# A linear-attention and feed-forward kernel on one core: the same steps in a new program order, 94 of them on another engine

## The chip, the cores and the metric

The kernel runs on one core of a Trainium2 chip. The metric is the device time of one execution in microseconds (us); the median of three runs before the change is 522.75 us (522.26 to 524.58).

## What is computed

Two stages follow one another. The first is a linear attention with a decaying state, for 4 batches, 8 heads, 768 time steps and a head dimension of 48. The second is a feed-forward layer over all 3072 tokens, from 384 to 2048 channels and back.

```python
for t in range(S):
    cur = np.einsum('bhd,bhe->bhde', u[None] * kt, vt)
    y[:, :, t] = np.einsum('bhd,bhde->bhe', rt, state + cur)
    state = w[None, :, :, None] * state + np.einsum('bhd,bhe->bhde', kt, vt)
...
h = x @ w_in
sp = np.maximum(h, 0.0) + np.log1p(np.exp(-np.abs(h)))
g = h * erf(sp)
return (g @ w_out).astype(np.float32)
```

## The kernel before

**Chunks.** Time is cut into chunks of 128 steps; 6 chunks of 4 batches make 24 chunk steps g = 0 to 23, each with all 8 heads. For a chunk the inputs r, k and v are loaded (`load_a`, `load_b`: words `L`), scaled by powers of the decay (`K`, `R`, `N`: lines 218, 222, 226), multiplied on TensorE into the in-chunk matrix A (`A`, L301), masked into two tiles am whose diagonal was prepared before (`Q` L263, L266, L270, then `M` L281 or L283, then `P` L309), and multiplied with v and with the state sbd into y (`Y`, L330). `D` (L353) with `S` (L366, L368, L372) moves the state on. `X` puts y into x in two parts, a rounded one and its residue (L375, L378; for chunks 0 to 3 through L389 and L392).

**Blocks.** Four chunks make a block x of 512 tokens; there are 6. For each block the feed-forward layer goes over 16 tiles of 128 hidden channels: 96 steps n. `f` (L411) is nine matmuls of 512 columns into h; `a b z c d e g` is the activation (ScalarE L418, L422, L431, L435, L439; VectorE L427, L443); `h` and `l` split the result into two parts (L449 on ScalarE, L454 on VectorE); `p` (L471) is nine matmuls into the three accumulators. The tile h has three buffers. Blocks 0 and 1 take turns: tiles 0 to 7 of both, then 8 to 15 of both; their sums go through memory in between (`O`).

**Weights.** The weights arrive as 64-bit words and are turned into two float parts on the chip, in 16 groups `Cwg` (w = 0 for w_in, 1 for w_out; g = 0 to 7; a group serves two hidden tiles). Part a (L123) is ScalarE's, b, c and d are three passes of VectorE over 128x768 (L125, L127, L130), e is a copy on ScalarE (L133), and f a subtraction (L135) on VectorE or GpSimd. All groups share one work tile wt and two raw tiles. `F` loads a group. By their shapes a raw tile is 768 KB, `load_a` brings 512 KB, `load_b` 608 KB (224 KB for chunks 0 and 1), and ub is 192 KB.

**The order.** `ORDER` (from line 701) is a table of words written out by hand or by a planner; the loop at lines 517 to 596 takes them one after another and issues each word's instructions on their engines. So the table is the program order of every engine's queue. The letter is the step, the number its chunk or hidden tile, and the last sign the engine of the steps that can run on several: none is VectorE, `+` is GpSimd, `*` is ScalarE (line 518):

```python
eng = {"+": nc.gpsimd, "*": nc.scalar}.get(x[-1], nc.vector)
```

`W2` issues two dummy matmuls (`keep_warm`, L92); ahead of the table 16 more are issued. Loads wait on SyncE's queue, in the table's order, for their buffers.

Of the kernel before, what the change touches and what calls it, by code (L numbers as in the profile page):

```python
# [36 lines left out]
V0, K0, R0, AW = 1024, 1472, 1856, 2240  # L37
# [669 lines left out]
M50* N4+ z2 M51 A5 C02b C02c C02d K6+ c2 f3 d2 a3 e2 e1 C02e p0x p0y p0z P50 g2 h2 b3 Q6a P51 g1 z3 C02f+ Q6b+ R6+ Y4
X4a D4 h1 c3 X4b l2 Q6c l1 C11a d3 L7a L7b F03 Y5 f4 f5 M60* X5a M61* e3 C11b C11c N5 C11d S4b S4a X5b C11e F12 R7+
C11f g3 Q7a+ K7+ Q7b+ a4 a5 b5 z5 b4 C03a c5 A6 p1 z4 P60 P61 p2 D5 Y6 C03b C03c C03d c4 d5 h3 l3 d4 e5 L8a L8b F13 g5
C03e X6a h5 e4 S5b S5a X6b Q7c p3 C03f+ M70+ C12a M71* A7 l5 g4 f6 f7 h4 a6 P70 C12b C12c C12d P71 Y7 l4 b6 C12e a7 b7  # L710
C12f z6 z7 C13a c6 c7 d6 X7a d7 e6 C13b C13c C13d X7b g6 N6+ K8+ Q8a+ F14 p4 p5 f8 e7 h6 g7 h7 C13e l6 a8 C13f l7 Q8b+
b8 z8 C14a C14b f9 a9 c8 b9 d8 C14c R8 S4c+ N7+ z9 Q8c M80+ e8 g8 p6 F04 p7x O70a c9 d9 h8 C14d l8 f10 a10 p7y e9 b10
g9 z10 M81+ A8 p7z f11 p8x P80 P81 N8+ O71a C14e c10 C14f+ S4d O70b F05 h9 O71b l9 O72a d10 e10 a11 b11 C05a D6 D7 p8y
p8z p9 f12 g10 h10 S7a S6a z11 C05b C05c c11 d11 e11 C05d C05e g11 h11 l10 l11 S7b O72b L10a L10b L9a L9b F07 a12 b12
C05f+ S6b z12 f13 f14 p10 C04a C04b C04c C04d p11 Y8 c12 a13 b13 d12 F15 e12 g12 z13 a14 C04e C04f b14 z14 h12 l12
# [118 lines left out]
```

## Time and profile before

| | |
|---|---|
| median of 3 runs | 522.75 us (522.26 to 524.58) |
| the profiled execution, its own time | 521.7 us |
| its span | 520.0 us |
| TensorE busy | 500.6 us (96%) |
| ScalarE busy | 392.8 us (76%) |
| VectorE busy | 361.2 us (69%) |
| GpSimd busy | 142.0 us (27%) |
| memory read and written | 41.09 MB and 6.29 MB |
| mean granted TensorE clock | 0.995 of full speed |

The span runs from the first to the last event of the core; the execution's own time lies 1.7 us above it. PE is TensorE, DVE is VectorE, ACT is ScalarE, POOL is GpSimd, SP is SyncE. A busy time is the part of the span in which an engine has an instruction under way; neighbouring instructions of one engine can overlap by some hundredths of a microsecond.

### The profile page before, as it was taken

What the parts mean: (1) busy time and instruction counts of PE and PEld (TensorE: products, weight loads), DVE (VectorE), ACT (ScalarE), POOL (GpSimd) and SP (SyncE); (2) the same over time, 40 slices, a digit from 0 to 9 for tenths busy, and PEclk for the clock granted to TensorE, in tenths of its full rate; (3) what the DMA queues carried; (4) which work ended last, traced back from release to release, by engine and by line L of the source; (5) the groups of instructions that cost most, each with busy time, mean ns of one, the idle gap of its engine ahead of it and who ended that gap; (6) DMA issues with size and microseconds to landing.
All of it is one profiled execution on the core that took longest, in us unless ns stands there. A gap on an engine that the chain in (4) does not pass through costs nothing.

```text
span 520.0 us, 11077 instructions
## 1 busy us (share of the span) xinstructions
PE 500.6 (96%) x4479; PEld 393.6 (76%) x4482; DVE 361.2 (69%) x636; ACT 392.8 (76%) x720; POOL 142.0 (27%) x139
## 2 busy tenths in 40 slices
PE   8888899999999999999999999999999999999995
PEld 4766667778777787877778787787777886888884
DVE  7999999997798865766467765657758655444452
ACT  2667859998998776777775877667787687887892
POOL 5444670423570323145312420113422000000000
PEclk9998999999999999999999999999999999999999
DMA  7853543561621142430203200514030000010001
GB/s 281 296 195 110 210 152 121 201 221 63 224 87 40 43 136 84 150 110 0 89 3 126 110 6 0 179 29 151 21 129 1 1 1 3 0 62 0 1 0 66
DMA packets 13993, 48.16 MB, mean 93 GB/s; under 512 B 1776, under 2 KB 2160, under 8 KB 13936
## 3 DMA queue, kind: packets, MB, share of 16 engines
q1 hardware_dynamic: 13936, 47.39, 26.0%
q8 instruction: 37, 0.61, 0.5%
q14 instruction: 20, 0.16, 0.1%
HBM read 41.09 MB, written 6.29 MB: 91 GB/s over the span
## 4 chain that ended last, share of the span: by engine, by line
PE 86%; DVE 7%; issue 2%; ACT 2%; POOL 1%; ACTq 0%; DVEq 0%; POOLq 0%
PE acc L471 39%; PE h L411 35%; PE y L330 5%; PE A L301 4%; PE dummy L92 1%; PE ds L353 1%; DVE wt L127 1%; DVE wt L130 1%; DVE am L309 1%; DVE wt L125 1%; DVE h L443 1%; DVE s L427 0%; POOL wil L135 0%; DVE att L218 0%; ACT x L375 0%
## 5 line engine op out<-in xcount | busy, mean ns | idle before, releaser
L411 PE MATMUL h<-x,wih 128*128 128x512 f32 x576 | 184.9, 402 | 2.4 <-DVE sbd L366 1.2
L411 PEld LDWEIGHTS h<-x,wih 128*128 128x128 f32 x576 | 107.4, 189 | 31.7 <-ACT x L375 1.3
L471 PE MATMUL acc<-gh,woh 128*128 128x512 f32 x288 | 117.0, 406 | 0.0
L411 PE MATMUL h<-x,wil 128*128 128x512 f32 x288 | 114.3, 397 | 0.0
L471 PE MATMUL acc<-gh,wol 128*128 128x512 f32 x288 | 114.2, 397 | 0.0
L471 PE MATMUL acc<-gl,woh 128*128 128x512 f32 x288 | 114.0, 396 | 0.0
L443 DVE SCALAR_TENSOR_TENSOR h<-s,h 128x512 f32<-128x512 f32 x96 | 66.3, 693 | 47.6 <-ACT s L439 47.1
L427 DVE SCALAR_TENSOR_TENSOR s<-s,h 128x512 f32<-128x512 f32 x96 | 65.1, 682 | 46.8 <-ACT s L422 46.6
L454 DVE TENSOR_TENSOR gl<-h,gh 128x512 fp32r<-128x512 f32 x96 | 66.1, 688 | 35.5 <-ACT gh L449 34.4
L449 ACT CAST gh<-h 128x512 fp32r<-128x512 f32 x96 | 56.0, 583 | 41.6 <-DVE h L443 31.0
L418 ACT ACTIVATE s<-h 128x512 f32<-128x512 f32 x96 | 56.8, 595 | 25.0 <-PE h L411 24.7
L431 ACT ACTIVATE s<-s 128x512 f32<-128x512 f32 x96 | 59.6, 627 | 20.2 <-DVE s L427 19.8
L471 PEld LDWEIGHTS acc<-gh,woh 128*128 128x128 f32 x288 | 54.2, 188 | 14.6 <-issue 0.8
L411 PEld LDWEIGHTS h<-x,wil 128*128 128x128 f32 x288 | 54.4, 189 | 13.1
L471 PEld LDWEIGHTS acc<-gh,wol 128*128 128x128 f32 x288 | 54.2, 188 | 13.2
L471 PEld LDWEIGHTS acc<-gl,woh 128*128 128x128 f32 x288 | 54.3, 189 | 12.0
L435 ACT ACTIVATE s<-s 128x512 f32<-128x512 f32 x96 | 60.2, 628 | 1.7
L422 ACT ACTIVATE s<-s 128x512 f32<-128x512 f32 x96 | 60.1, 630 | 1.8
L439 ACT ACTIVATE s<-s 128x512 f32<-128x512 f32 x96 | 60.1, 630 | 1.6
L283 POOL TENSOR_TENSOR am<-idents,q 128x512 f32<-128x512 f32 x24 | 27.9, 1168 | 98.9 <-DVE q L270 49.0
L309 DVE COPY_PREDICATED am<-mask,A 64x128 f32<-64x128 uint32 (+2 forms) x108 | 38.3, 389 | 2.3 <-PE A L301 1.5
L330 PE MATMUL y<-am,att 128*32 128x128 f32 x768 | 26.7, 273 | 4.0 <-DVE am L309 2.3
(89 smaller groups left out, 482.2 us busy)
## 6 DMA issues: line engine op xcount, KB each, us to landing
att<-in_att_dram SPq DMA_DIRECT2D x22, 608.0 KB, 5.7
att<-in_att_dram SPq DMA_DIRECT2D x24, 512.0 KB, 4.1
raw<-in_win_dram SPq DMA_DIRECT2D x8, 768.0 KB, 6.1
raw<-in_wout_dram SPq DMA_DIRECT2D x8, 768.0 KB, 4.6
out_dram<-o SPq DMA_DIRECT2D x18, 256.0 KB, 2.1
part<-o SPq DMA_DIRECT2D x6, 256.0 KB, 2.4
o<-part SPq DMA_DIRECT2D x6, 256.0 KB, 4.4
att<-in_att_dram SPq DMA_DIRECT2D x2, 224.0 KB, 7.4
```

Source lines behind the costliest of these rows:

```text
L330: nc.tensor.matmul(out=y[r:r + 32, q, :], lhsT=lhsT, rhs=rhs, start=r not in new, stop=True, skip_group_check=True)
L411: nc.tensor.matmul(out=h, lhsT=w[:, f, q, :], rhs=x[:, xi, q, :], start=k == 0, stop=k == 8)
L418: nc.scalar.activation(out=s1, in_=e["h"], func=AF.Tanh, bias=FB0, scale=FA0)
L422: nc.scalar.activation(out=s1, in_=s1, func=AF.Tanh, bias=FB1, scale=FA1)
L427: nc.vector.scalar_tensor_tensor(out=e["s"], in0=e["s1"], scalar=FG, in1=e["h"], op0=ALU.mult, op1=ALU.add)
L431: nc.scalar.activation(out=s, in_=s, func=AF.Tanh, bias=FB2, scale=FA2)
L435: nc.scalar.activation(out=s, in_=s, func=AF.Square, bias=FB3, scale=FA3)
L439: nc.scalar.activation(out=s, in_=s, func=AF.Square, bias=FB4, scale=FA4)
L443: nc.vector.scalar_tensor_tensor(out=h, in0=ff[n]["s"], scalar=FC, in1=h, op0=ALU.subtract, op1=ALU.mult, reverse0=True)
L449: nc.scalar.copy(out=e["gh"], in_=e["h"])
L454: eng.tensor_tensor(out=e["gl"], in0=e["h"], in1=e["gh"].bitcast(F32), op=ALU.subtract)
L471: nc.tensor.matmul(out=acc[e], lhsT=w[:, f, es], rhs=g, start=first and i == 0, stop=last and i == 2)
```

## The change

Only the table changes: the loop, the steps and all shapes stay. The new table holds the same words in another order, but for three `W2` of nine, which are gone (6 dummy matmuls). 94 words carry another engine sign: of the steps `N`, `K`, `R`, `Qa`, `Qb`, `M`, `S` and `C..f`, 42 go from GpSimd to VectorE and 5 to ScalarE, 36 come to GpSimd from VectorE and 7 from ScalarE, and 4 change between VectorE and ScalarE. Two lines of each table:

```diff
-L0a W2 W2 W2 L1a U0 L0b L2a L2b L3a L3b L1b F00 B0 B0* F01 K0 R0 A0 K1 G0 R1 V0 A1 G1 P00 K2+ V1 Q0 P01 P10 T0 H0 N0*
-t0 N1* Y0 D0 D1 Q2a+ R2 Q2b Q3a Q3b+ R3+ Q2c P11 M20+ Q1 M21* S0d Q3c Y1 C00a X0a M30* L4a L4b S0c S1c S1d C00b N3
+L0a L0b L1a F00 L2a L2b L1b L3a U0 L3b B0 B0* C00a R2+ R0 K0 A0 G0 V0 R1 K1 F01 G1 C00b P00 P01 C00c Q0 A1 W2 V1 C00d
+Q1 P10 P11 R3+ N0* H0 C00e Y0 D0 W2 T0 X0a N1* t0 Y1 D1 L5a L5b Q2a+ S0c Q3a Q2b Q2c M20* S0d K2 X1a M21* A2 L4a Q3b
...
```

**SyncE, the first loads.** Before, all of the first four chunks is loaded ahead of the first weights (raw00 is group C00):

```order
L68 DMA att0_167<-in_att_dram 128x1024
L68 DMA att1_178<-in_att_dram 128x1024
L81 DMA ub_90<-in_u_dram 128x384
L72 DMA att0_167<-in_att_dram 128x448
L68 DMA att2_182<-in_att_dram 128x1024
L72 DMA att2_182<-in_att_dram 128x1216
L68 DMA att3_185<-in_att_dram 128x1024
L72 DMA att3_185<-in_att_dram 128x1216
L72 DMA att1_178<-in_att_dram 128x448
L107 DMA raw00_189<-in_win_dram 128x768
```

After:

```order
L68 DMA att0_167<-in_att_dram 128x1024
L72 DMA att0_167<-in_att_dram 128x448
L68 DMA att1_170<-in_att_dram 128x1024
L107 DMA raw00_172<-in_win_dram 128x768
L68 DMA att2_174<-in_att_dram 128x1024
L72 DMA att2_174<-in_att_dram 128x1216
L72 DMA att1_170<-in_att_dram 128x448
L68 DMA att3_178<-in_att_dram 128x1024
L81 DMA ub_90<-in_u_dram 128x384
L72 DMA att3_178<-in_att_dram 128x1216
```

The first weights move from the tenth to the fourth of these loads, and the loads of chunks 2 and 3 and of ub stand behind them.

**GpSimd, from the preparation of chunk 7 to that of chunk 8** (att7 and att8 are the chunks' inputs, wol and wil the second weight parts, am the masks). Before:

```order
L263 TENSOR_TENSOR att7_807<-att7_807,ub_90 128x384
L218 TENSOR_TENSOR att7_807<-att7_807,wk_116 112x512
L266 TENSOR_TENSOR att7_807<-att7_807 128x384
L135 TENSOR_TENSOR wil_95<-wt03_897,wih_94 128x768
L283 TENSOR_TENSOR am7_0_1023<-idents_98,q7_1011 128x512
L226 TENSOR_TENSOR att6_579<-att6_579,wkn_146 128x384
L218 TENSOR_TENSOR att8_997<-att8_997,wk_116 112x512
L263 TENSOR_TENSOR att8_997<-att8_997,ub_90 128x384
L266 TENSOR_TENSOR att8_997<-att8_997 128x384
L372 TENSOR_TENSOR sbd_147<-sbd_147,wp_114 48x4x48
L226 TENSOR_TENSOR att7_807<-att7_807,wkn_146 128x384
```

After:

```order
L263 TENSOR_TENSOR att7_811<-att7_811,ub_90 128x384
L135 TENSOR_TENSOR wol_97<-wt11_861,woh_96 128x768
L218 TENSOR_TENSOR att7_811<-att7_811,wk_116 112x512
L226 TENSOR_TENSOR att7_811<-att7_811,wkn_146 128x384
L226 TENSOR_TENSOR att6_554<-att6_554,wkn_146 128x384
L283 TENSOR_TENSOR am7_0_987<-idents_98,q7_984 128x512
L283 TENSOR_TENSOR am7_1_989<-idents_98,q7_984 128x512
L135 TENSOR_TENSOR wol_97<-wt12_1038,woh_96 128x768
L266 TENSOR_TENSOR att8_976<-att8_976 128x384
L218 TENSOR_TENSOR att8_976<-att8_976,wk_116 112x512
```

The five steps on chunk 8, the state and chunk 7 that followed one another are split: those of chunk 7 come earlier, and those of chunk 8 stand behind the subtraction for weight group C12 (wt12), which needs VectorE's passes over that group.

**VectorE, the passes over C12 and the masks of chunk 7** (wt12 is C12's work tile, am7 the masks). Before:

```order
L454 TENSOR_TENSOR gl_5_1050<-h5_851,gh_5_1005 128x512
L443 SCALAR_TENSOR_TENSOR h4_841<-s2_4_927,h4_841 128x512
L309 COPY_PREDICATED am7_0_1023<-mask_99,A7_0_1032 128x512
L125 TENSOR_SCALAR wt12_1025<-wt12_1025 128x768
L127 SCALAR_TENSOR_TENSOR wt12_1025<-raw12_881,wt12_1025 128x768
L130 SCALAR_TENSOR_TENSOR wt12_1025<-raw12_881,wt12_1025 128x768
L309 COPY_PREDICATED am7_1_1027<-mask_99,A7_1_1033 128x512
L454 TENSOR_TENSOR gl_4_1111<-h4_841,gh_4_1073 128x512
L135 TENSOR_TENSOR wol_97<-wt12_1025,woh_96 128x768
```

After:

```order
L135 TENSOR_TENSOR wil_95<-wt03_949,wih_94 128x768
L454 TENSOR_TENSOR gl_4_1034<-h4_873,gh_4_1020 128x512
L427 SCALAR_TENSOR_TENSOR s2_5_1036<-s1_5_1017,h5_951 128x512
L125 TENSOR_SCALAR wt12_1038<-wt12_1038 128x768
L127 SCALAR_TENSOR_TENSOR wt12_1038<-raw12_978,wt12_1038 128x768
L130 SCALAR_TENSOR_TENSOR wt12_1038<-raw12_978,wt12_1038 128x768
L427 SCALAR_TENSOR_TENSOR s2_6_1053<-s1_6_1050,h6_1024 128x512
L309 COPY_PREDICATED am7_0_987<-mask_99,A7_0_991 128x512
L309 COPY_PREDICATED am7_1_989<-mask_99,A7_1_992 128x512
```

The subtraction for C03 (wil), on which the matmuls of hidden tiles 6 and 7 rest, is now VectorE's and stands eight instructions ahead of the second mask of chunk 7; before it was GpSimd's.

## Rows read from the trace of the kernel before

**Rows 1.** Busy time by stretches: from-to, length, then each engine's busy us (instructions), PEclk.
```profile
60.00:80.00 20.00, 17.36 (x253) 13.54 (x253) 19.22 (x26) 13.87 (x27) 11.77 (x10) 1.00 0.43 144
80.00:100.00 20.00, 20.00 (x176) 15.31 (x172) 18.99 (x32) 19.41 (x35) 5.60 (x4) 1.00 0.43 151
...
320.00:360.00 40.00, 39.69 (x441) 31.56 (x441) 25.98 (x49) 28.52 (x52) 6.78 (x7) 1.00 0.34 117
...
400.00:440.00 40.00, 39.16 (x366) 30.97 (x358) 23.57 (x45) 29.09 (x55) 2.36 (x2) 1.00 0.01 2
```

**Rows 2.** Chain that ended last, in order of time: start us, us, what.
```profile
44.76 3.18 PE h L411 x9
...
247.00 2.10 PE h L411 x9
249.11 1.67 PE y L330 x56
```

**Rows 3.** Timeline of PE around 79 us: start us, us, what [idle before <-releaser].
```profile
79.14 1.07 PE L330 MATMUL y<-am,att 128*32 128x128 f32 x28 [2.25 <-DVE am L309]
...
80.13 0.50 PE L471 MATMUL acc<-gh,woh 128*128 128x512 f32 x1
```

**Rows 4.** Timeline of DVE, 54 to 82 us: the passes of two weight groups and neighbours.
```profile
54.42 0.55 DVE L125 TENSOR_SCALAR wt<-wt 128x768 int32<-128x768 int32 x1
55.00 0.96 DVE L127 SCALAR_TENSOR_TENSOR wt<-raw,wt 128x768 int32<-128x768 int32 x1
...
56.35 3.03 DVE L130 SCALAR_TENSOR_TENSOR wt<-raw,wt 128x768 int32<-128x768 int32 x1
...
72.26 2.35 DVE L125 TENSOR_SCALAR wt<-wt 128x768 int32<-128x768 int32 x1
74.65 1.67 DVE L127 SCALAR_TENSOR_TENSOR wt<-raw,wt 128x768 int32<-128x768 int32 x1
76.35 2.10 DVE L130 SCALAR_TENSOR_TENSOR wt<-raw,wt 128x768 int32<-128x768 int32 x1
78.37 0.71 DVE L309 COPY_PREDICATED am<-mask,A 128x512 f32<-128x512 uint32 x1
```

**Rows 5.** Timeline of POOL, 71 to 78 us, first and last of five.
```profile
71.93 1.29 POOL L218 TENSOR_TENSOR att<-att,wk 112x512 f32<-112x512 f32 x1
...
76.64 0.99 POOL L226 TENSOR_TENSOR att<-att,wkn 128x384 f32<-128x384 f32 x1
```

**Rows 6.** Timeline of DVE, 28 to 47 us: first and last of four more long instructions.
```profile
28.98 1.77 DVE L218 TENSOR_TENSOR att<-att,wk 112x512 f32<-112x512 f32 x1
...
44.80 1.63 DVE L125 TENSOR_SCALAR wt<-wt 128x768 int32<-128x768 int32 x1
```

**Rows 7.** Groups by line and shape: line engine op xcount | busy us, mean ns | idle before.
```profile
L443 DVE SCALAR_TENSOR_TENSOR h<-s,h 128x512 f32<-128x512 f32 x96 | 66.3, 693 | 47.6 <-ACT s L439 47.1
L427 DVE SCALAR_TENSOR_TENSOR s<-s,h 128x512 f32<-128x512 f32 x96 | 65.1, 682 | 46.8 <-ACT s L422 46.6
L135 DVE TENSOR_TENSOR wol<-wt,woh 128x768 fp32r<-128x768 f32 x5 | 4.8, 961 | 0.9 <-ACT woh L133 0.9
L283 DVE TENSOR_TENSOR am<-idents,q 128x512 f32<-128x512 f32 x6 | 4.3, 716 | 0.0
L226 DVE TENSOR_TENSOR att<-att,wkn 128x384 f32<-128x384 f32 x7 | 3.8, 551 | 0.0
L231 DVE TENSOR_TENSOR att<-att 112x512 f32<-112x512 f32 x2 | 1.4, 688 | 0.0
```

**Rows 8.** Timeline of POOL, its first large step.
```profile
10.19 1.54 POOL L218 TENSOR_TENSOR att<-att,wk 112x512 f32<-112x512 f32 x1 [4.99 <-DMA att<-in_att_dram]
```

**Rows 9.** Busy time of PE alone by stretches of 2 us: PE busy, PEclk.
```profile
44.00:46.00 2.00, 2.00 (x17) 0.50 0.83 335
```

**Rows 10.** Timeline of PE and DVE: six dummies, and masks late in the span.
```profile
39.16 1.89 PE L92 MATMUL dummy<-warm 128*128 128x512 bf16 x6 [0.27 <-PE h L411]
...
433.13 1.94 DVE L309 COPY_PREDICATED am<-mask,A 128x256 f32<-128x256 uint32 x6
```

More of the change, by code (lines that the diff above doesn't have):

```diff
@@ L707 @@
[L707 to L711, printed above, removed]
@@ new lines @@
+C00f Q3c M30* M31* K3+ P20 N3+ A3 X0c X1c Q5a K5 X1b X0b C01a P30 P31 D3 Y3 L4b P21 Y2 Q5b+ S1d Q5c S1c Q4a N2+ D2 X3a
+X2a R4+ C01b Q4b K4 S3d Q4c M40+ M41+ C01c S3c S2d C01d S2c F02 L6a L6b F10 X3c X2c X3b X2b W2 f0 A4 f1 M50* M51* a0
+b0 z0 C01e C01f f2 Q6a N4 P40 P41 Q6b+ R5+ A5 W2 K6+ R6+ c0 d0 a1 e0 b1 g0 z1 a2 b2 z2 h0 l0 C10a P50 C10b C10c C10d
+P51 Q6c f3 c2 c1 d2 e2 Y4 D4 W2 C10e X4a d1 C10f C02a N5 X4b C02b C02c S4a C02d Y5 W2 p0x p0y p0z L7a F11 F03 L7b e1
+a3 X5a b3 C02e R7+ C02f+ X5b g1 S4b h1 M60* M61+ A6 g2 z3 l1 C11a c3 d3 h2 e3 P60 C11b C11c C11d P61 f4 C11e a4 D5 Y6
@@ new lines @@
+p1 Q7a+ C11f+ b4 S5b g3 l2 X6a C03a f5 p2 K7+ z4 S5a X6b C03b L8a F12 C03c Q7b N7+ C03d Q7c N6+ M70+ M71+ A7 c4 h3 d4
+e4 l3 g4 a5 C03e h4 b5 C03f f6 l4 z5 C12a c5 C12b C12c C12d L8b F14 F13 d5 a6 b6 z6 P70 e5 P71 g5 f7 C12e a7 p3 Y7
+C12f+ Q8a b7 c6 z7 h5 d6 l5 e6 X7a c7 d7 e7 Q8b+ Q8c g6 X7b K8+ M80+ M81+ g7 p4 p5 f8 h6 l6 C13a C13b h7 C13c C13d l7
+a8 b8 z8 C13e f9 f10 c8 a9 d8 b9 z9 S4d+ C13f+ R8+ e8 C14a F05 g8 C14b C14c p6 c9 a10 d9 h8 C14d l8 p7x p7y p7z A8 e9
+C14e b10 O70a O70b F04 g9 O71a h9 f11 C14f+ P80 z10 l9 C05a a11 c10 b11 C05b P81 d10 O72a e10 z11 C05c g10 C05d p8x
@@ new lines @@
+p8y f12 D6 D7 p8z O71b L9a L9b F15 O72b L10a p9 c11 a12 d11 h10 l10 e11 g11 C05e C05f b12 z12 h11 l11 f13 p10 f14 p11
+C04a c12 a13 d12 b13 e12 C04b C04c C04d F07 z13 g12 C04e c13 h12 l12 d13 S6a K10+ C04f+ a14 e13 g13 b14 z14 h13 l13
+S7a f15 f16 C07a c14 p12 Q9a C07b C07c C07d a15 d14 b15 z15 e14 F06 g14 a16 C07e b16 z16 h14 l14 c15 C07f+ d15 e15 g15
+S5d p13 f17 p14 C15a h15 c16 a17 d16 e16 b17 C15b l15 C15c C15d g16 F16 L10b z17 S7b p15x C15e h16 l16 p15y f18 f19
+p15z c17 O150a d17 S7c+ S5c+ C15f+ S4c+ Y8 Q9b N8 S6b D8 p16x C06a a18 b18 e17 C06b C06c C06d g17 O151a a19 b19 z19
@@ new lines @@
+h17 l17 O150b z18 Q9c O152a c19 p16y p16z O152b F17 L11a L11b O230a O151b O231a p17 C06e d19 e19 c18 S8b C06f f20
+Q10a+ g19 d18 h19 l19 e18 R10+ S8d+ Q10b+ C16a g18 h18 C16b l18 a20 f21 f22 b20 z20 a21 c20 d20 b21 e20 p18 C16c C16d
+S8a Q11a g20 Q10c z21 a22 C16e h20 l20 b22 z22 c21 d21 c22 d22 e22 N9+ M90+ R9+ C16f+ g22 p19 f23 e21 h22 a23 g21 l22
+p20 f24 b23 z23 h21 l21 C17a C17b C17c C17d f25 c23 d23 e23 C17e a25 p21 K9 C17f g23 a24 b25 z25 h23 l23 X8a b24 S6c+
+M91+ Q11b+ X8b z24 p22 p23x p23y A9 S7d O230b Q11c c24 M100+ d24 c25 d25 e24 P90 P91 f26 p23z Y9 g24 h24 e25 l24 g25
@@ new lines @@
+h25 a26 X9a f27 R11 l25 O231b X9b b26 M101 a27 b27 p24x A10 M110+ z26 O230c O232a c26 d26 e26 O232b K11 P100 N10+ N11
+P101 g26 M111+ f28 a28 p24y p24z b28 z28 h26 l26 z27 c27 d27 p25 A11 f29 e27 a29 P110 P111 Y11 D11 g27 h27 l27 c28 d28
+b29 X11a e28 p26 X11b z29 S11b S11a g28 c29 d29 h28 S6d l28 L12a L12b O231c f30 D9 Y10 L13a O310a O232c L13b p27 p28
+f31 a30 b30 e29 Q12a+ K12+ Q12b Q12c z30 M120+ g29 h29 c30 X10a S9a d30 e30 a31 b31 N12 M121+ R12+ X10b S9b A12 l29
+Q13a+ S8c+ Q13b+ f32 P120 O311a P121 Y12 D12 g30 Q13c z31 h30 a32 b32 z32 c31 p29 d31 X12a e31 S12b l30 M130 g31 X12b
@@ new lines @@
+a40 f41 p37 p38 A14 b40 z40 d39 e39 g39 c40 d40 a41 h39 R16+ M150+ R15 l39 N15 b41 e40 P140 g40 h40 z41 l40 p39 f42
+f43 p40 c41 d41 e41 a42 b42 M151 S10c g41 P141 z42 c42 h41 d42 a43 e42 b43 l41 g42 h42 K15+ l42 z43 A15 f44 a44 b44
+c43 p41 p42 f45 d43 P150 Q16b z44 P151 e43 c44 d44 g43 e44 g44 h44 N16 l44 a45 b45 h43 Y15 Y14 f46 z45 l43 Q16c M160+
+c45 X15a a46 b46 z46 d45 X14a c46 d46 e46 f47 p43 p44 X14b X15b g46 e45 h46 g45 h45 l46 a47 b47 l45 D14 D15 f48 a48
+p45 S15b z47 c47 d47 b48 e47 z48 g47 c48 h47 l47 d48 S14a p46 f49 L17a L17b O311c L18a L18b O312c e48 a49 g48 h48 b49
@@ new lines @@
+e56 h55 l55 a57 b57 L20a L20b L19a g56 z57 h56 l56 L19b S15d+ Q19a+ Q19b+ K19+ S18b S16c R19 f58 c57 X18a f59 a58 d57
+e57 b58 z58 p55 p56 a59 b59 g57 h57 c58 S18a X18b z59 d58 e58 c59 l57 Q19c S15c+ M190 Q20a Q20b+ S18c+ M191* g58 h58
+l58 A19 f60 a60 d59 e59 b60 p57 p58 f61 P190 z60 K20+ P191 g59 c60 d60 e60 h59 N19 g60 h60 a61 b61 D17 S17a S17b l60
+l59 z61 Y19 D19 f62 f63 c61 d61 e61 a62 a63 b62 b63 X19a p59 g61 S19a Q20c h61 z63 z62 c63 c62 l61 d62 d63 e62 L21a
+L21b O470b L23a L23b S18d+ R23+ Q23a+ K23 X19b S16d+ Q21a S17d+ Q21b+ Q23b+ M200+ g62 p60 p61 f64 e63 h62 M201+ g63
@@ new lines @@
+h63 l62 a64 b64 S19b l63 z64 f65 a65 f66 c64 b65 d64 e64 p62 Q21c z65 g64 Q23c R20 M210 c65 d65 a66 b66 z66 h64 l64
+p63x p63y p63z A20 f67 e65 O630a O631a c66 g65 P200 P201 p64x Y20 O630b h65 d66 e66 l65 a67 b67 O632a g66 z67 L22a
+O631b O632b L22b c67 M211* f68 p64y p64z p65 a68 X20a h66 d67 l66 e67 b68 g67 z68 c68 h67 l67 X20b Q22a+ K22+ R21+
+S19c+ K21+ R22+ f69 p66 f70 a69 b69 d68 e68 Q22b z69 g68 Q22c c69 a70 h68 l68 b70 d69 M220+ p67 e69 z70 g69 c70 A21
+f71 d70 e70 h69 a71 b71 P210 P211 M221* S17c+ l69 g70 z71 c71 d71 p68 f72 p69 A22 e71 a72 b72 h70 g71 h71 S19d l70 l71
@@ new lines @@
+f73 P220 z72 c72 a73 b73 d72 e72 g72 P221 z73 f74 a74 p70 Y21 Y22 p71 b74 c73 d73 e73 h72 M230+ X22a M231+ g73 l72 h73
+z74 X22b l73 f75 c74 a75 b75 d74 X21a f76 a76 e74 p72 X21b g74 z75 h74 c75 b76 l74 z76 A23 p73 c76 d76 e76 d75 e75
+P230 P231 g75 h75 l75 g76 p74 f77 Y23 Z0 f78 a77 b77 z77 h76 X23a l76 c77 f79 p75 p76 d77 e77 a78 b78 z78 g77 X23b a79
+c78 d78 h77 l77 e78 g78 f80 b79 h78 z79 l78 c79 d79 e79 a80 b80 g79 z80 f81 a81 b81 z81 p77 p78 c80 h79 l79 d80 e80
+c81 g80 h80 d81 l80 p79x f82 e81 a82 O790a p79y f83 b82 z82 g81 O791a c82 p79z p80x p80y a83 h81 l81 b83 z83 O790b
@@ new lines @@
+O792a c83 d83 e83 O791b O792b f84 d82 p80z g83 h83 l83 e82 g82 p81 f85 a84 h82 b84 l82 z84 a85 b85 z85 c84 p82 p83 f86
+c85 d85 e85 g85 d84 h85 l85 e84 g84 h84 a86 l84 b86 z86 f87 a87 p84 f88 p85 b87 z87 c86 d86 e86 g86 c87 d87 h86 l86
+e87 a88 g87 b88 z88 h87 l87 f89 c88 a89 d88 b89 z89 e88 g88 p86 p87 f90 c89 h88 d89 e89 l88 g89 h89 l89 a90 b90 z90
+f91 f92 a91 c90 d90 b91 z91 e90 a92 b92 g90 p88 p89 z92 h90 l90 c92 d92 e92 c91 f93 p90 g92 h92 d91 l92 e91 g91 a93
+b93 z93 h91 l91 f94 f95 c93 p91 d93 a94 b94 z94 e93 g93 a95 c94 b95 d94 z95 h93 l93 p92 e94 c95 g94 d95 h94 l94 e95
@@ L765 @@
+g95 p93 h95 l95 p94 p95x O950a p95y O951a p95z O952a O950b O951b O952b
 """
```

66 lines of the change are left out of this document (10 added, 56 removed).

## The prediction

> **What bounds the kernel now.** I read the busy times by stretches first. From 80 us on TensorE has work without a gap: 20.00 of 20 us, and later 39.69 and 39.16 of 40 [rows 1]. In the stretch before that it is VectorE that is full, 19.22 of 20 us, while TensorE has 17.36 [rows 1]. The chain of waits in order of time says the same: after 80 us it runs over lines 411, 471 and 330 of TensorE, piece behind piece [rows 2]. So the kernel has two parts: an early one in which VectorE prepares attention and weights and TensorE waits for it, and a late one in which only TensorE's own work counts. What the change is worth is read in the early part, and then in the few gaps of the late one.
>
> I take one place as the border: the first product of hidden tile 4, `p4`. It starts at 80.13 us, behind `Y7`, which waited 2.25 us for the second mask of chunk 7 on VectorE (finished at 78.37 + 0.71 = 79.08) [rows 3, 4]. In both tables `p4` is word 299, and TensorE's words ahead of it are the same (8 A, 8 Y, 6 D, 8 f, 6 p and the small ones) but for the `W2`. So behind `p4` the same TensorE work is left, and the change in time is the shift of `p4` plus what the late gaps gain or lose.
>
> **The change part by part.**
>
> *VectorE's load.* Up to the second mask of chunk 7 VectorE has 101 steps in both tables. Their kinds differ: `C..f` 4 for 2, `Qa`/`Qb` 8 for 5, `z` 7 for 6; `M` none for 2, `N` 2 for 3, `R` 2 for 4, `g` 5 for 6. With 0.96 us for `C..f`, 0.55 for `Q` and `N` (one shape), 0.72 for `M`, 0.69 for `R` (the shape of L231) and for `g`, and 0.68 for `z` [rows 7], that is +1.92 +1.65 +0.68 -1.44 -0.55 -1.38 -0.69 = **+0.2 us**. So many steps change engine, and VectorE has as much to do as before. ScalarE's words sum to the same there too. GpSimd has 24 steps for 22.
>
> *The gate moves forward.* Before, the last thing that TensorE waited for was that mask. In the new table the matmuls of hidden tiles 6 and 7 wait for the subtraction of C03, now VectorE's, and they stand so close to `p4` that only f6, f7, p3 and Y7 follow: 3 x 2.10 + 1.67 = 8.0 us [rows 2]. VectorE has eight instructions from that subtraction to the mask: about 5.4 us (0.55, 0.96, 0.96 for the clean passes [rows 4], the rest 0.6 to 0.7 each, less 0.08 us each by which neighbours overlap: L125 at 54.42 for 0.55 us and L127 at 55.00, for instance, against L127 to L125 at 74.65 and 72.26 where they don't). Then `p4` comes 8.0 us after C03f, where by the mask it would come 5.4 + 80.13 - 79.08 = 6.4 us after it. That costs up to **+1.6 us**.
>
> *Waits between VectorE and GpSimd.* Some VectorE instructions take much longer where GpSimd runs. The pass L130 took 3.03 us, against 0.96 for L127 of the same shape nearby; L125, L127 and L130 of C12 took 2.35, 1.67 and 2.10, against 0.55, 0.96 and 0.96, while five GpSimd steps ran back to back from 71.93 to 77.63 [rows 4, 5]. That is 2.07 us and 3.65 us; four more instructions between 28 and 47 us lost 3.2 us together [rows 6], so 8.9 us in all ahead of `p4`. VectorE's L443 and L427, which read a PSUM tile, have means of 0.69 and 0.68 over 96, no more than clean ones [rows 7]. The Trainium skill, page "SBUF — State Buffer", section "Who interferes with whom", names the mechanism: the two engines share a port pair that is held for a whole instruction, by VectorE when it reads two SBUF inputs or runs in a two-port mode. The rows agree. By that rule alone, with any GpSimd step that reads SBUF able to block a pass, nothing is relieved and the sum below would be rival 1's, +4.1 us; by the runs that the rows show it is +0.7.
>
> The new GpSimd order takes away the run of five beside C12: the steps on chunk 8 now stand behind the subtraction of C12, which needs those passes finished. Those 3.65 us go. In their place two `N` steps of 0.99 us [rows 5] stand beside the passes of C03; I let one of them block. Ahead of C03f the loss is then 8.9 - 3.65 + 1.0 = 6.3 us, so **-2.6 us** (ends: 4 us left, -4.9, and 9.7 us left, +0.8, the old loss in proportion to GpSimd's steps, 24 for 22).
>
> *The first weights.* VectorE's first pass over C00 now stands seventh in its attention work. Its load is the fourth of the large ones, behind 512 + 224 + 512 KB: 2,016 KB with itself. Before, GpSimd waited till 10.19 us for the load that brought the sum to 1,952 KB [rows 8]. So it lands at about 10.3 us, ScalarE's part a takes 0.9, and VectorE, free at about 10.4, waits **+0.8 us** (0 to 0.8). The loads of chunks 2 and 3 move back by the same 768 KB; their steps come later in the table, so I put nothing on them.
>
> *Six dummies fewer.* Six took 1.89 us [rows 10]. They lay in time in which TensorE waited for VectorE: 0 (0 to -1.5). What they covered: at 44 to 46 us the granted clock was 0.50, which is the 1.2 GHz level, after TensorE had been little busy, and nine matmuls took 3.18 us instead of 2.10 [rows 2, 9]. One more such fall costs 0 while TensorE waits anyway, 1.1 us if not; I take 0.
>
> *The late gaps.* Before, TensorE lacks 0.31 and 0.84 us in the two late stretches [rows 1]. Masks for a late chunk keep VectorE 1.94 us [rows 10]; where only one group of nine matmuls (2.10 us) stands between A and Y, nothing may come between. Before that holds at chunks 19 and 23; now at 11 and 12, and with 2.8 us at 9 and 20. Two more such places at 0.31 to 0.84: **+0.7 us** (-0.5 to +2.3).
>
> **Sum.** 0.2 + 1.6 - 2.6 + 0.8 + 0 + 0.7 = +0.7 us on the profiled execution's 521.7 us (its span of 520.0 and 1.7 around it), so 522.4. That execution stands 1.05 us below the median of 522.75, and so I predict a median of **523.4 us**: no change that can be told. About 0.5%, 2.6 us, is what a measurement of this kernel can tell from no change.
>
> **Rivals.**
>
> 1. *The waits between VectorE and GpSimd are not relieved* (slower). The runs of GpSimd only change their partners: 24 steps for 22 ahead of the gate, with K7, N7, N6 and two `M` in front of C03f. If they block as the old ones did per step (9.7 us), the sum becomes 0.2 + 1.6 + 0.8 + 0.8 + 0.7 = +4.1, a median of 526.9. For it: the loss before was 0.4 us per GpSimd step wherever it fell. Against it: two thirds of it lay in two runs beside weight passes. It decides once more than about 8 us are lost ahead of C03f. Chance 0.20.
> 2. *Masks come late* (slower). Chunks 9, 11, 12 and 20 each lose what the worst late stretch lost, 0.84 us: +3.4 in place of +0.7, a median of 526.1. For it: at chunk 12 a VectorE step of 0.7 us stands between. Against it: the same distance cost only 0.31 at chunk 19. Chance 0.12.
> 3. *The early part becomes shorter* (faster). Only 4 us are lost ahead of C03f and the first weights cost nothing: then `p4` is bounded by 0.2 + 1.6 - 4.9 = -3.1, the late gaps stay, and the median is 519.7. For it: the worst run is dissolved and the second, 2.07 us, changes its partners too. Against it: more of GpSimd's work comes before the gate. Chance 0.30.
>
> The forecast keeps 0.38. That gives faster 0.30, within 0.5% 0.38, slower 0.32. As cases of both signs hold most of the chance: the forecast's own range is 520.5 to 525.3. The whole range reaches to rival 3 with dummies worth 1.2 us more (518.5) and to rival 1 with a fall of the clock and a late gap more (528.6); beyond it lie about 2 in 10.
>
> **What would show it.** In the new profile: `p4` between 79 and 81.5 us; TensorE full from there, with gaps of 1 to 2.5 us in all up to 500 us; f6 waiting for line 135 on VectorE; VectorE's L125, L127 and L130 of C12 near 0.55 and 0.96; VectorE's first L125 starting near 11.2 us behind ScalarE; means over all 16 of L130 below 1.25 us. The prediction is wrong if `p4` shifts by over 2.6 us, or if TensorE has gaps of over 3 us behind it.

## The result, and the profile after

The new table takes **515.25 us** (median, 513.87 to 515.58) where the old one took 522.5 us on the same chip (521.0 to 524.58): a ratio of 0.985, 95% interval [0.982, 0.989], 1.5% faster. The prediction was 523.4 us with a range from 518.5. The profiled execution took 513.87 us, its span is 511.8 us: 8.2 us less than the profiled span before.

`p4` starts at 73.82 us, 6.31 us earlier than before; what stands behind it takes 437.98 us in place of 439.87. So three quarters of the gain lie ahead of the border.

Timeline of TensorE in the new profile (start us, us, what, in brackets the idle time before it and what ended it):

```profile
56.42 0.86 PE L330 MATMUL y<-att,sbd 112*32 112x128 f32 x24 [0.86 <-DVE am L309]
...
65.63 0.74 PE L411 MATMUL h<-x,wih 128*128 128x512 f32 x2
66.20 0.40 PE L411 MATMUL h<-x,wil 128*128 128x512 f32 x1
...
72.15 0.86 PE L330 MATMUL y<-att,sbd 112*32 112x128 f32 x24
72.83 1.06 PE L330 MATMUL y<-am,att 128*32 128x128 f32 x32
73.82 0.50 PE L471 MATMUL acc<-gh,woh 128*128 128x512 f32 x1
```

The 2.25 us in front of `Y7` [rows 3] are gone. The last wait is 0.86 us in front of `Y6`, and from 56.42 us TensorE is full: between that wait and `p4` stand `Y6`, `p1`, `f5`, `p2`, `A7`, `f6`, `f7`, `p3` and `Y7`, 17.4 us of work.

Timeline of VectorE, to be held against [rows 4, 6]; the last four rows are the passes over C12 and the masks of chunk 7:

```profile
11.28 0.56 DVE L125 TENSOR_SCALAR wt<-wt 128x768 int32<-128x768 int32 x1 [0.93 <-ACT wt L123]
...
17.75 1.63 DVE L266 TENSOR_TENSOR att<-att 128x384 f32<-128x384 f32 x1
...
55.65 0.72 DVE L309 COPY_PREDICATED am<-mask,A 128x512 f32<-128x512 uint32 x1
...
64.83 1.08 DVE L135 TENSOR_TENSOR wil<-wt,wih 128x768 fp32r<-128x768 f32 x1
...
67.02 1.21 DVE L125 TENSOR_SCALAR wt<-wt 128x768 int32<-128x768 int32 x1
68.27 0.96 DVE L127 SCALAR_TENSOR_TENSOR wt<-raw,wt 128x768 int32<-128x768 int32 x1
69.26 0.96 DVE L130 SCALAR_TENSOR_TENSOR wt<-raw,wt 128x768 int32<-128x768 int32 x1
...
70.73 1.36 DVE L309 COPY_PREDICATED am<-mask,A 128x512 f32<-128x512 uint32 x2
```

The passes over C12 take 3.13 us where they took 6.12, and the masks end at 72.09 in place of 79.08. The row at 55.65 is the second mask of chunk 6, for which `Y6` waits. L266 at 17.75 us (clean 0.55) and L125 at 67.02 us are the only instructions there that still lose 0.5 us or more.

Timeline of GpSimd in the same stretch:

```profile
48.62 1.70 POOL L222 TENSOR_TENSOR att<-att,wr 112x512 f32<-112x512 f32 x1 [7.47 <-DMA att<-in_att_dram]
...
56.44 1.02 POOL L263 TENSOR_TENSOR att<-att,ub 128x384 f32<-128x384 f32 x1 [3.34 <-DMA att<-in_att_dram]
...
62.46 2.62 POOL L226 TENSOR_TENSOR att<-att,wkn 128x384 f32<-128x384 f32 x2 [1.96 <-DVE att L266]
65.06 2.76 POOL L283 TENSOR_TENSOR am<-idents,q 128x512 f32<-128x512 f32 x2
71.16 1.84 POOL L135 TENSOR_TENSOR wol<-wt,woh 128x768 fp32r<-128x768 f32 x1 [3.35 <-ACT woh L133]
```

Its pauses are 41.1 to 48.6, 53.1 to 56.4, 60.5 to 62.5 and 67.8 to 71.2 us, and in each of them VectorE has passes of a weight group, of two groups in the first. Its queue waits there for a load, for VectorE, or for ScalarE's copy of C12. The busy times of the stretches of passes show it. Columns: from-to, length, busy us of PE, PEld (TensorE's weight loads), DVE, ACT, POOL, then granted clock, DMA share and GB/s. First the last of seven stretches before, the passes over C12, and the sum of the seven:

```profile
72.26:78.45 6.19, 4.62 (x44) 3.39 (x42) 6.12 (x5) 1.30 (x3) 5.29 (x5) 1.00 0.15 60
sum 28.53, PE 25.46 PEld 18.40 DVE 28.21 ACT 14.75 POOL 14.04; mean PE 3.64 PEld 2.63 DVE 4.03 ACT 2.11 POOL 2.01
```

The same after:

```profile
67.02:70.22 3.20, 3.20 (x16) 2.56 (x15) 3.13 (x5) 2.91 (x5) 0.79 (x1) 1.00 0.00 0
sum 23.46, PE 23.15 PEld 17.94 DVE 23.02 ACT 16.25 POOL 6.70; mean PE 3.31 PEld 2.56 DVE 3.29 ACT 2.32 POOL 0.96
```

Beside the passes GpSimd is busy 6.70 us in place of 14.04, at C12 0.79 in place of 5.29.

Behind the border two stretches of [rows 1] read now:

```profile
320.00:360.00 40.00, 40.00 (x388) 32.57 (x388) 26.81 (x51) 30.31 (x56) 15.08 (x16) 1.00 0.26 95
400.00:440.00 40.00, 40.00 (x348) 32.27 (x347) 20.76 (x39) 29.96 (x54) 2.04 (x2) 1.00 0.01 2
```

From 80 to 480 us TensorE lacks 1.25 us before and 0.20 after.

### The profile page after: what moved, and what is told of

Read it like the earlier page. It is cut to its first block, busy times and chain, and to the rows that moved or that the text cites. A ratio compares the mean times of both kernels' runs of the same rounds, so it can differ in the third digit from the quotient of the medians.

```text
span 511.8 us, 11055 instructions
## 1 busy us (share of the span) xinstructions
PE 496.6 (97%) x4476; PEld 391.8 (77%) x4476; DVE 357.4 (70%) x642; ACT 390.4 (76%) x712; POOL 135.7 (27%) x135
## 4 chain that ended last, share of the span: by engine, by line
PE 85%; DVE 5%; DMA 4%; ACT 3%; SPq 1%; issue 1%; ACTq 0%
PE acc L471 38%; PE h L411 37%; PE y L330 6%; PE A L301 3%; DMA out_dram<-o 2%; DMA raw<-in_win_dram 1%; PE ds L353 1%; DMA att<-in_att_dram 1%; DVE wt L130 1%; DVE wt L127 1%; DVE am L309 1%; DVE gl L454 1%; ACT s L435 0%; SPq L72 0%; ACT s L422 0%
## 5 line engine op out<-in xcount | busy, mean ns | idle before, releaser
L454 DVE TENSOR_TENSOR gl<-h,gh 128x512 fp32r<-128x512 f32 x96 | 66.0, 689 | 39.8 <-ACT gh L449 38.3
L283 POOL TENSOR_TENSOR am<-idents,q 128x512 f32<-128x512 f32 x25 | 28.5, 1150 | 76.6 <-PE y L330 65.5
L222 POOL TENSOR_TENSOR att<-att,wr 112x512 f32<-112x512 f32 x16 | 21.8, 1363 | 42.8 <-DMA att<-in_att_dram 42.8
```

Of the source, the lines that this page charges most:

```text
L454: eng.tensor_tensor(out=e["gl"], in0=e["h"], in1=e["gh"].bitcast(F32), op=ALU.subtract)
```

## The experiments

For each kernel I add up VectorE's time ahead of the second mask of chunk 7 and take off the same instructions at the mean durations that they have in the kernel without GpSimd (below). What is left is called the **loss**; "idle" is VectorE's idle time there.

| kernel | `p4` at | loss | idle | median us | ratio to old |
|---|---|---|---|---|---|
| old, first profile | 80.13 | 9.2 | 3.3 | 522.5 | |
| old, again | 79.74 | 8.9 | 3.2 | 522.69 | 1.001 [0.998, 1.005] |
| old to `p4`, then new | 81.28 | 8.6 | 4.2 | 521.78 | 0.997 [0.993, 1.001] |
| old, C12's subtraction on GpSimd | 81.30 | 7.4 | 5.3 | 525.25 | 1.002 [0.998, 1.007] |
| old, no GpSimd ahead of `p4` | 82.93 | 0.0 | 1.8 | 526.4 | 1.005 [1.001, 1.008] |
| new, first profile | 73.82 | 2.4 | 2.6 | 515.25 | 0.985 [0.981, 0.989] |
| new, again | 75.19 | 2.5 | 3.7 | 514.61 | 0.983 [0.979, 0.988] |
| new to `p4`, then old | 75.05 | 2.4 | 3.8 | 519.34 | 0.993 [0.990, 0.997] |
| new, a run put back at C12 | 75.88 | 3.9 | 3.6 | 515.26 | 0.983 [0.977, 0.989] |
| new, a pause filled | 75.80 | 3.2 | 4.6 | 516.73 | 0.988 [0.984, 0.992] |
| new, six more dummies | 76.83 | 2.6 | 5.4 | 517.0 | 0.988 [0.984, 0.992] |
| new, no GpSimd ahead of `p4` | 86.52 | 0.3 | 4.3 | 528.17 | 1.011 [1.007, 1.014] |

**Order and engine signs apart.** The new order with the old signs, and the old order with the new signs; one place of the first:

```diff
-Q6a N4 P40 P41 Q6b+ R5+ A5 W2
+Q6a N4+ P40 P41 Q6b+ R5 A5 W2
```

> The new order, with every step on the engine it had before. Theory (the gain is VectorE time no longer lost to GpSimd's port; which passes stand beside which GpSimd steps decides): the order alone changes the partners, so most of the lock loss stays away, p4 at 74 to 77 us and 515 to 518 us. Rival (the engine moves carry the gain): 521 to 524 us.

> The old order, with every step on the engine that it has in the new table. Theory: GpSimd's runs stand where the old order puts them, though of other steps, so part of the 8.9 us stays: 519 to 524 us. Rival (the engine moves carry the gain): 515 to 517 us.

Measured: 561.68 us (ratio 1.072 [1.065, 1.079]) and 546.27 us (1.044 [1.036, 1.052]). Every expectation missed. Steps land on engines whose queues stand elsewhere. In the first of the two the granted clock was also 0.50 from 12 to 28 us, a cost of its own that these runs don't separate. With the new order and old signs, the waits of VectorE over the span begin to show what goes wrong (total us, times, longest):

```profile
DVE q L270 <- POOL att L266: 6.9, 2, 3.9
...
DVE att L222 <- DMA att<-in_att_dram: 5.4, 1, 5.4
```

`R2`, which GpSimd can wait with, now holds VectorE's queue 5.4 us for its load. The order and the signs are one thing and can't be valued apart.

**Ahead of the border and behind it.**

```diff
 (words 0 to 298 of the new table)
-p4 p5 f8 h6 l6 C13a C13b h7 ...
+C13a C13b C13c C13d p4 p5 f8 h6 h7 C13e ...
```

and the reverse, the old table up to `p4` and the new order behind it. What one table issues ahead of `p4` and the other behind it goes to the seam: four steps on C13 in the first, and in the second seven steps (N7, e7, Q8b, Q8c, M80, M81, g7) that stand just ahead of `p4`.

> The new table up to p4, and from there the old table's order. Theory: p4 at about 74 us as in the new kernel, the late gaps of the old one (1.2 us instead of 0.2): 515 to 517.5 us. Rival (a good part of the gain lies behind p4): 518 us and more.

> The old table up to p4, and from there the new table's order. Theory: p4 at about 80 us as before, late gaps as in the new kernel: 520 to 522.5 us. Rival (a good part of the gain lies behind p4): below 519 us.

With the new early part `p4` comes at 75.05 us; with the old one it comes at 81.28 (with `Y7` at a granted clock of 0.50), and the new late order alone brings no gain that can be told. The first missed its time by 2 us and lies with 519.34 where the rival had put it: what stands behind `p4` takes 442.15 us, 2.3 us more than before. At the seam `f` waits 2.4 us for the second part of an activation (L454), and the old late order's wait of 0.8 us near its end is back. So by `p4` the gain is made ahead of the border; by the times it is not shown alone, as a late part has to be made for it.

**GpSimd taken away.** In both tables the steps of GpSimd ahead of `p4` become VectorE's (25 in the old, 26 in the new, where R2, R3 and N3 stay):

```diff
-Q5b+ C10f+ Q5c P41 l0 C02a M50* N4+ ...
+Q5b C10f Q5c P41 l0 C02a M50* N4 ...
```

> The old table with all 25 steps of GpSimd that stand ahead of hidden tile 4 put on VectorE. By clean durations VectorE gets about 14.5 us more to do ahead of the second mask of chunk 7. Theory (8.9 us of VectorE's time there were waits beside GpSimd): the waits vanish with their partner, so the first product of hidden tile 4 comes only about 5 to 6 us later, at 85 to 86.5, and L125, L127 and L130 have clean means of 0.55 to 0.6, 0.96 and 0.96; time 526 to 529. Rival (the long instructions are long by themselves or wait for something else): 13 to 15 us later, at 93 to 95, time 534 to 538.

> The new table with the 26 steps of GpSimd ahead of hidden tile 4 put on VectorE, but for the three that would make it wait for a load or for ScalarE (R2, R3, N3). By clean durations that is about 14 us more ahead of the same mask. Theory (the new order left only about 2 us of waits there): the first product comes 11 to 13.5 us later than 73.82, at 85 to 87.5, near the place that the old table without GpSimd gives; time 526 to 529.5. So GpSimd's help would be worth about twice as much in the new order as in the old. Rival (the new order is shorter by its order of VectorE's work, not by fewer waits): the product comes 5 to 8 us later, at 79 to 82, some 5 us ahead of the old table without GpSimd; time 520 to 523.

The groups of VectorE in the old table without GpSimd, from 6 to 87 us (count | busy us, mean ns | idle):

```profile
L130 DVE SCALAR_TENSOR_TENSOR wt<-raw,wt 128x768 int32<-128x768 int32 x8 | 7.7, 956 | 0.2
L127 DVE SCALAR_TENSOR_TENSOR wt<-raw,wt 128x768 int32<-128x768 int32 x8 | 7.6, 954 | 0.2
...
L125 DVE TENSOR_SCALAR wt<-wt 128x768 int32<-128x768 int32 x8 | 4.4, 550 | 0.0
```

Every pass is clean. Up to 79.05 us of the old profile L130, L127 and L125 had means of 1.41, 1.12 and 0.96. This shows whose doing the long passes are. 22 more instructions stand ahead of the mask, some 15 us by their durations, and `p4` comes only 2.8 us later, or 3.2 against the second old profile (I had expected 5 to 6, and had not taken off the 0.08 us by which each instruction overlaps its neighbour, 1.8 us in all, nor the 1.5 us that VectorE idles less). In the new table it comes 11.3 to 12.7 us later, as the theory said. Some 1.6 us of that may be the clock's: here `f3` ran at a granted clock of 0.50 to 0.64 and took 3.84 us for 2.30, and behind it VectorE waited 0.79 and 0.78 us that neither profile of the new table has. **So GpSimd's help ahead of `p4` was worth some 3 us in the old table, and is worth 10 to 13 us in the new one.** The rival, that VectorE's order makes the new table short, falls: without GpSimd the new table's `p4` is the later one.

**The run at C12 taken out, and put in.** In the old table one sign, which puts an instruction that needs the passes in front of the steps on chunk 8 in GpSimd's queue; in the new table the reverse (with the load of chunk 8's second part named earlier):

```diff
-C12e a7 b7 C12f z6 z7
+C12e a7 b7 C12f+ z6 z7
```

```diff
-N6+ M70+ M71+ A7 ...
+N6+ M70+ M71+ K8+ Q8a+ Q8b+ R8+ A7 ...
```

> The old table with one sign changed: the subtraction of C12 goes from VectorE to GpSimd, at its old place. GpSimd's steps on chunk 8 (N6, K8, both Qs) then stand in its queue behind an instruction that needs VectorE's passes over C12, as in the new table. Theory (VectorE's long passes are GpSimd's doing, and the queue that runs ahead of the table brings them together): L125, L127, L130 of C12 fall from 2.35, 1.67, 2.10 to about 0.55 to 0.7, 0.96, 0.96, the second mask of chunk 7 comes some 3.5 us earlier, and the first product of hidden tile 4 comes 1 to 2.3 us earlier than 80.13 (TensorE then waits for nothing there, or for the slower subtraction); time 520 to 521.5. Rival (the passes were long for another reason, or the gain comes from the order of VectorE's work): the passes keep about 6.1 us together, the product stays at 80 to 81, time 522 to 523.

> The new table with four steps on chunk 8 (K8, both Qs, R8; one Q from VectorE, all on GpSimd) put back ahead of the passes of C12, right behind the diagonal work on chunk 7, and the load of chunk 8's second part named earlier so that it stands ahead of them. Theory (a run of GpSimd beside the passes makes them wait): L125, L127, L130 of C12 take 4.5 to 6.5 us together where they took 3.13, the masks of chunk 7 come 1.5 to 3 us later, the first product of hidden tile 4 comes 1 to 3 us later than 73.82; time 516 to 518.5. Rival: the passes stay near 3.1 us, the product within 0.5 us of 73.8, time 515 to 515.5.

In the old table the passes become clean:

```profile
76.07 0.54 DVE L125 TENSOR_SCALAR wt<-wt 128x768 int32<-128x768 int32 x1
76.64 0.96 DVE L127 SCALAR_TENSOR_TENSOR wt<-raw,wt 128x768 int32<-128x768 int32 x1
77.63 0.96 DVE L130 SCALAR_TENSOR_TENSOR wt<-raw,wt 128x768 int32<-128x768 int32 x1
```

`Y7` waits for nothing, and from `A6` on `p4` comes 18.66 us later where it came 19.75 us later: 1.1 us gained there. But in this execution `A6` itself stood 2.3 us later (62.64 against 60.38; L263 took 2.04 us and L226 2.63, ahead of anything that the edit touches). The 1.1 us are also too few for what was cured: the granted clock was 0.50 to 0.85 at 62 to 68 us, and `A6` and the two `p` behind it took 7.26 us for 5.69. And the run was not gone. It stood beside the next group, C13, whose passes are clean in both old profiles and took 1.67, 1.65 and 1.64 us here:

```profile
82.53 1.67 DVE L125 TENSOR_SCALAR wt<-wt 128x768 int32<-128x768 int32 x1 [0.80 <-ACT wt L123]
```

Behind them `f8` waits 2.06 us for x. No gain in the time: one cured place is not the table.

In the new table with the run, VectorE and GpSimd:

```profile
68.05 1.21 DVE L125 TENSOR_SCALAR wt<-wt 128x768 int32<-128x768 int32 x1
69.30 1.93 DVE L127 SCALAR_TENSOR_TENSOR wt<-raw,wt 128x768 int32<-128x768 int32 x1
71.26 1.65 DVE L130 SCALAR_TENSOR_TENSOR wt<-raw,wt 128x768 int32<-128x768 int32 x1
```

```profile
68.80 1.61 POOL L218 TENSOR_TENSOR att<-att,wk 112x512 f32<-112x512 f32 x1
70.37 1.72 POOL L263 TENSOR_TENSOR att<-att,ub 128x384 f32<-128x384 f32 x1
72.17 1.61 POOL L266 TENSOR_TENSOR att<-att 128x384 f32<-128x384 f32 x1
```

The passes take 4.79 us for 3.13, and TensorE has two new waits, 0.80 us at `Y7` and 0.27 us inside `p4`: 1.1 us, of the 1 to 3 expected. The median is 515.26 us on another chip, in the rival's range; against its own old runs it can't be told from the new table. So the trace shows the collision, and the time does not show its price.

**Both tables once more.** No edit.

> The old table unchanged, for a second profile and the spread of its times. Three profiles of the old early part (the kernel before and two experiments that share it) lost 9.2, 8.6 and 7.4 us of VectorE's time ahead of the second mask of chunk 7, against the durations without GpSimd, but at different instructions. Theory (which instruction is hit is a matter of a few tenths of a microsecond, how much is lost in all is a matter of the table): again 7 to 9.5 us, with other long instructions than in the first profile; the first product of hidden tile 4 at 79 to 82; time 521 to 526. Rival (the places are fixed by the table): the same long instructions, L130 of the fifth group and all three passes of C12, within 0.3 us each.

> The new table unchanged, for a second profile and for comparison on the same chip. Theory: the loss ahead of the mask is 2 to 3.5 us again, because the passes stand in GpSimd's pauses (its queue waits there for loads, for VectorE or for ScalarE); the first product of hidden tile 4 at 73.5 to 75.5; time 514 to 517. Rival (the new profile was a lucky one): 5 us or more lost, product after 77.

The old one, passes over C12:

```profile
71.89 2.34 DVE L125 TENSOR_SCALAR wt<-wt 128x768 int32<-128x768 int32 x1
74.27 1.66 DVE L127 SCALAR_TENSOR_TENSOR wt<-raw,wt 128x768 int32<-128x768 int32 x1
75.96 2.09 DVE L130 SCALAR_TENSOR_TENSOR wt<-raw,wt 128x768 int32<-128x768 int32 x1
```

These are the rows of before [rows 4] within 0.01 us. My theory of wandering places falls, at least here: the table fixes the group and nearly the sum (in the fifth group of passes L130 took 1.77 us for 3.03 and L226 in front of it 1.65 for 0.55, which is not within the rival's 0.3 us). Its 12 runs spread from 520.3 to 528.1 us, the 6 of the new one from 513.8 to 515.5; why is not shown.

The new one loses 2.5 us again, so its small loss was no luck. Its `p4` stood at 75.19, 1.4 us later than in the first profile. What differs is the granted clock: 0.50 to 0.71 at 22 to 30 us here, 1.00 there. The matmuls of `A` for two chunks, in the first profile and in this one:

```profile
21.33 1.98 PE L301 MATMUL A<-att 48*64 48x128 f32 x64 [1.13 <-DMA att<-in_att_dram]
21.61 3.06 PE L301 MATMUL A<-att 48*64 48x128 f32 x64 [0.82 <-DMA att<-in_att_dram]
```

The passes over C10 start at 42.33 us here and at 40.75 there, and the other profiles of the new early part fall into the same two groups: 42.21 and 42.16 with such a fall (the old late order, the run at C12), 40.53 and 40.69 without (the pause and the dummies, below). So a fall at that place costs 1.4 to 1.8 us. Between the two second profiles `p4` moves by 4.55 us (79.74 to 75.19) and the span by 6.3 (519.6 to 513.3): less than between the first two, and again some three quarters of it ahead of the border.

**A pause filled, and dummies.** Two steps of VectorE go into GpSimd's pause of 7.5 us; and, apart from it, three dummy words are added:

```diff
-D4 W2 C10e X4a d1 C10f C02a N5 X4b
+D4 W2 C10e X4a d1 C10f+ C02a N5+ X4b
```

```diff
-Q6b+ R5+ A5 W2 K6+ ... P51 Q6c f3
+Q6b+ R5+ A5 W2 K6+ ... P51 Q6c W2 W2 W2 f3
```

> The new table with two steps of VectorE (the subtraction of C10, 0.94 us, and N5, 0.54 us) given to GpSimd, where it has a pause of 7.5 us from 41.1 to 48.6 us. VectorE has 1.5 us less to do. Theory (the pauses are what keeps VectorE's passes clean): GpSimd now runs beside the passes of C02 (46.5 to 49.1), VectorE loses 0.8 to 2 us there, and the mask and the first product of hidden tile 4 stay within 0.7 us of the new table's; time within 1 us of it. Rival (GpSimd's time in a pause is free): the product comes 1.2 to 1.6 us earlier and the time is 1.2 to 1.6 us less.

> The new table with three more dummy words (six matmuls of about 0.3 us) ahead of f3, where TensorE waits 0.79 us for VectorE and soon after 0.86 us more. The prediction's term for dummies was zero: they lie in time in which TensorE waits for VectorE. Theory: they fill those waits; the first product of hidden tile 4 moves by 0 to 0.5 us, time within 1 us of the new table's on the same chip. Rival (TensorE's own work counts there): both 1.6 to 1.9 us later.

The filled pause costs 2.1 us against the new table on the same chip (516.73 and 514.61), where theory said less than 1 and the rival a gain. VectorE, passes over C02:

```profile
47.14 0.56 DVE L125 TENSOR_SCALAR wt<-wt 128x768 int32<-128x768 int32 x1 [1.86 <-ACT wt L123]
47.74 0.96 DVE L127 SCALAR_TENSOR_TENSOR wt<-raw,wt 128x768 int32<-128x768 int32 x1
...
48.87 1.78 DVE L130 SCALAR_TENSOR_TENSOR wt<-raw,wt 128x768 int32<-128x768 int32 x1
```

L130 loses 0.83 us as expected. What I had not counted is the 1.86 us: all groups share the tile wt, so ScalarE's part for C02 can't begin until the subtraction of C10 has read it, and on GpSimd that subtraction ends at 46.1 us (44.29 + 1.83) where VectorE's ended at 45.5. Against the first profile the second mask of chunk 6 ends 1.5 us later (57.90 and 56.37) and `p4` comes 2.0 us later; the other 0.5 us is `f4`, which ran at a granted clock of 0.55 to 0.59 here and took 3.8 us for 2.3.

The dummies cost 2.4 us (517.0). The waits that I meant them to fill stand elsewhere: in the new profile the 0.79 us are in front of `f4` and the 0.86 in front of `Y6`, and in front of `f3` TensorE waits for nothing. So `f3` starts 1.65 us later than in the first profile (41.90 and 40.25) and `p4` 3.0. The rival is right that TensorE's own work counts there, as later steps of VectorE hang on it (VectorE idles 5.4 us in place of 2.6 and 3.7). But the cost is above the rival's 1.6 to 1.9 us, and `f4` ran at a granted clock of 0.50 to 0.67 here too (3.8 us for 2.3); its share was not told apart, and dummies that lie in a wait were not tried.

## Why the prediction was wrong

The mechanism was named rightly and mis-sized by more than half. Against the second mask of chunk 7, which came 6.99 us earlier:

- **VectorE's load**, +0.2 predicted: the clean durations up to the mask sum to 66.7 us before and 67.3 after, +0.7. Right in kind.
- **First weights**, +0.8: L125 waits 0.93 us and starts at 11.28, as forecast (11.2). But VectorE's idle time as a whole falls by 0.7 us, because 1.1 us of waits for A are gone, which I had not looked at (in the second new profile it is 0.4 more than before).
- **Waits between VectorE and GpSimd**, -2.6 with 6.3 us left: this is the step that failed. 2.4 us are left, a change of -6.7 us, beyond my lower end of 4. I took away the run at C12 alone and kept each other loss as if it stayed at its instruction: 2.07 us at L130 and 3.2 us in the four of [rows 6]. None of these is left. What is lost now is 1.1 us at L266, 0.66 at L125 of C12 and little else: GpSimd's queue is held at other places, and all groups of passes changed their partners, not one. The two `N` beside C03 did not block (L127 and L130 there 0.96 and 0.95).
- **The gate**, up to +1.6: `p4` comes 7.91 us after the end of C03's subtraction (65.91), where 8.0 was forecast. The distance from mask to `p4` grew from 1.05 to 1.73 us: +0.7. VectorE needed 6.2 us from there to the mask in place of 5.4. But that the distance fits is in part luck, as neither C03's subtraction nor the masks of chunk 7 set `p4`: TensorE did not wait for line 135, as I had said it would (it came 0.3 us before it was needed), but was full from `Y6` on. What set `p4` was the second mask of chunk 6, done at 56.37, and 17.4 us of TensorE's own work.
- **Dummies**, 0: six put in front of `f3` of the new table, where TensorE has no wait, cost 2.4 us, a fall of the clock included. What the six of [rows 10] cost in the old table was not tried; TensorE's busy time ahead of `p4` fell by 3.4 us (67.93 to 64.53). The half clock of [rows 9] is not in the first new profile, but the second has a fall at 22 to 30 us with `p4` 1.4 us later. So a fall was not free, as I had taken it to be, though one came in most profiles of either table.
- **Late gaps**, +0.7: the sign was wrong, and the cause. I had read the 0.84 us of [rows 1] as a late mask. The trace of before says

```profile
439.61 0.50 PE L411 MATMUL h<-x,wih 128*128 128x512 f32 x1 [0.84 <-ACT x L375]
```

  It is `f80`, the first `f` of the last block, waiting for x of chunk 23. The old table has only `p76` between `Y23` and `f80`, the new one `f78`, `f79`, `p75` and `p76`. The wait is there with the old late order behind the new early part, and not with the new late order behind the old early part. The masks of chunks 9, 11, 12 and 20 cost nothing. In all the late part is 1.9 us shorter, 1.05 of it such gaps up to 480 us; of the rest, 0.6 us is less busy time of TensorE, which was not traced.

Rival 3 had the right side and too little: it let 4 us remain and kept the late gaps. Its sum with the measured terms is -6.99 + 0.68 - 1.89 = -8.2, the difference of the spans.

## What to carry to other kernels

A helper engine that shares a path with the busy one is worth what it does in the busy one's other moments: here some 25 steps were worth 3 us in one table and 10 to 13 us in the other, by where they stood. When a table is reordered, don't remove one collision and keep the rest, and look where the run goes that you move: in the old table it went from C12 to C13; lay the helper's queue anew, ask at each long pass what holds that queue back, and remember that a queue runs ahead of the table until something in it has to wait. Read each gap by the instruction behind it and its releaser before you put a cause to it. Before two executions are compared, compare their granted clock by stretches: one fall hid here as 1.4 us of scatter.

## What the runs showed of the hardware

VectorE's turn does not come at every end of a GpSimd instruction. In the old table with the new late order, L125 of C12 needs 0.55 us and took 4.30:

```profile
72.45 4.30 DVE L125 TENSOR_SCALAR wt<-wt 128x768 int32<-128x768 int32 x1
```

GpSimd beside it:

```profile
72.13 1.30 POOL L218 TENSOR_TENSOR att<-att,wk 112x512 f32<-112x512 f32 x1
73.37 1.03 POOL L263 TENSOR_TENSOR att<-att,ub 128x384 f32<-128x384 f32 x1
74.35 1.01 POOL L226 TENSOR_TENSOR att<-att,wkn 128x384 f32<-128x384 f32 x1
75.32 1.02 POOL L266 TENSOR_TENSOR att<-att 128x384 f32<-128x384 f32 x1
```

It sat through four instructions that overlap by about 0.05 us each, and went on when the last had ended at 76.34. In the kernel before the same L125 took 2.35 us: it got through at 74.2, where GpSimd's third step began 0.08 us after the second had ended. But a gap is not needed. Earlier in the same execution as the 4.30 us:

```profile
57.79 1.77 DVE L130 SCALAR_TENSOR_TENSOR wt<-raw,wt 128x768 int32<-128x768 int32 x1
```

```profile
57.53 1.21 POOL L263 TENSOR_TENSOR att<-att,ub 128x384 f32<-128x384 f32 x1
58.71 1.98 POOL L218 TENSOR_TENSOR att<-att,wk 112x512 f32<-112x512 f32 x1
```

L130 ended at 59.56, 0.82 us behind the end of L263 at 58.74, though L218 had begun 0.03 us before that end; and L218 took 1.98 us for its 1.30. Which engine goes on at such an end, no run here explains.

The Trainium skill, page "SBUF — State Buffer", section "Who interferes with whom", says that whoever comes first holds the shared ports for one whole instruction. The rows agree that the other side is blocked and not slowed (the L125 of 4.30 us ended 0.41 us behind the last of the four), and add that the same engine can hold them for several instructions in a row. GpSimd is kept waiting as well: its pair of L283 took 2.76 us at 65.06 in the new profile, beside VectorE's L135 and L125, and 2.05 us at 76.24, beside steps that read a PSUM tile.
